# Seven products of sums for the second products of a gated layer, on one Trainium2 core

## The chip, the core and the metric

The kernel runs on one core of a Trainium2 chip. Five engines matter: TensorE (PE in the profile, its weight loads PEld), VectorE (DVE), ScalarE (ACT), GpSimd (POOL) and SyncE (SP), which here only issues DMAs. Each works through its own list of instructions in order and waits on semaphores for the others. The metric is the device time in microseconds (us) of one execution; lower is better.

## The reference

Two layers, each an attention block and a gated block, on one sequence of 2048 tokens with 448 features, all in float32:

```python
x = x + _A_ref(_layernorm(x), A_wqkv, A_wo)              # attention, 16 heads of 28
x = x + _B_ref(_layernorm(x), B_w_gate, B_w_up, B_w_down)
# the same two lines once more, with the same weights

def _B_ref(x, w_gate, w_up, w_down):                     # (448,1792), (448,1792), (1792,448)
    g = jnp.einsum("bsd,df->bsf", x, w_gate)
    u = jnp.einsum("bsd,df->bsf", x, w_up)
    h = _sigmoid(g) * u
    return jnp.einsum("bsf,fd->bsd", h, w_down)
```

## The kernel before

**Precision.** Matmuls outside the mixing of values run in float16 on pairs: a value a is kept as `hi` = a rounded to float16 and `lo` = a - hi, and a product is three matmuls, hi·hi, hi·lo and lo·hi. `split` makes such a pair with one cast on ACT and one subtraction on DVE.

**Stages of a layer.** `project` makes queries, keys and values; `attend` goes through 16 heads; `out_project` applies the output weights and adds to x; `gated` is the gated block. Everything is issued in the order of the program text (`manual_schedule`), so each engine's queue is the order of these calls. During attention of layer 0 `Prepare` also splits the weights of the gated block on DVE, a step every few key tiles (`along`), and writes them to DRAM as `gu_parts` and `dn_parts`; `FEW` and `ASIDE` say how many score tiles of each head take their exponential on DVE (`score_aside`) and not on ACT (`score`).

**The gated stage.** The tokens lie in NB = 4 blocks of W = 512, the 1792 features in NP = 7 pairs of tiles of 128 (tile p and tile p + 7). The list `seq` goes through blocks b and, inside, pairs p. For each pair `gate_and_up` makes gate and up products by a scheme of seven products (the sums of the token side are made in the `half_steps` of the block, the sums of the weight side lie in `gu_parts`): 78 matmuls of 128x256 in PSUM banks 4 to 7. The two banks `chain` are copied out by ACT in between (`on_chain`, L1319), the two banks `side` are added in by DVE (`c11_c22` L1335, `c12` L1342). Then ACT applies the sigmoid (L1346), DVE multiplies (`times`, L1349), and `split` casts and subtracts h into two pairs of 128x512 (L200, L201). The second products of the pair before (`down`, L1288 to L1290) come next on PE: for each pair 24 matmuls of 128x448 into four banks `dnp` that gather over all seven pairs of a block; at its end DVE adds them to x (L1293). So on PE the order is gate and up of pair p, second products of pair p - 1, gate and up of pair p + 1.

**Fill.** Between pairs, `run_fill` calls the steps that make the next block's token operands: statistics and scaling (`norm`, `squares`, on DVE with a little on POOL), a turn through DRAM (`store`, `gather`), then seven steps that subtract and split (`half_steps`, L354 to L376, on DVE and ACT). Two steps a pair from pair 1 on. In the last block of layer 0 the fill makes the first block of the next layer.

**Weights.** `gu_parts` of a pair are two loads of 800 KB. Some pairs stay in SBUF from block to block, others are read again (`AFTER`, `used`, issued by POOL at L1243); `dn_parts` are loaded once a layer and stay. Large tiles come from 19 slots of SBUF (`big`) that are handed out in the order in which they were given back, small ones from 12 (`qrt`).

Of the kernel before, what the change touches and what calls it, by code (L numbers as in the profile page):

```python
# [19 lines left out]
P = 128  # L20
# [6 lines left out]
NB = 4  # L27
# [12 lines left out]
XS = 2.0 ** 10  # L40
PS = 2.0 ** -13
UNIT = 32768.0
VC = 32
# [62 lines left out]
def interleaved_layers(ctx: ExitStack, tc: tile.TileContext, x_in, wqkv, wo, w_gate, w_up,  # L106
# [729 lines left out]
    class Prepare:  # L836


        def __init__(self):
            nc.vector.memset(sums[:, 3:7], 0.0)  # L840
            self.part = cpool.tile([P, 2], F32, name="part", tag="part", bufs=1)
            self.raws, self.packs = big.ring(2), big.ring(2)
            self.halves = None
            tiles = [("o", 0)] + [("d", j) for j in range(4)] + [("gu", j) for j in range(7)]
            order = [(self.measure, what) for what in tiles] + [
                (self.split, what) for what in tiles[:5] + [(w, p) for p in range(NP)
                                                            for w in ("g", "u")]]
# [22 lines left out]
        def read(self, kind, j):  # L870
            if kind in "gu" and len(kind) == 1:
                if self.halves is None:
                    self.halves = big.at(self.raws, "raws", [P, 2, 1024])
                self.next = self.halves[:, (kind == "u") * 1]
            else:
                self.next = big.at(self.raws, "raw", [P, 2048])
            if kind == "o":
                load_rows(self.view(self.next, kind), wo, 0, D, nc.gpsimd)
            elif kind == "gu":
                for i, w in enumerate((w_gate, w_up)):  # L880
                    load_rows(self.view(self.next, kind)[:, i], w, j * 2 * P, 2 * P, nc.gpsimd)
            elif kind in "gu":
                v, w = self.view(self.next, kind), {"g": w_gate, "u": w_up}[kind]
# [15 lines left out]
        def view(self, t, kind):  # L899
            if kind == "gu":  # L900
                return t.rearrange("p (w s c) -> p w s c", w=2, s=4)
            if kind in "gu":
                return t[:, 0:1024].rearrange("p (s z n) -> p s z n", s=4, z=2)
            return t[:, 0:4 * D].rearrange("p (s n) -> p s n", s=4)

        def step(self, do, what, then):
            raw = self.next
            self.write()
            if then:
                self.read(*then)  # L910
            do(raw, *what)
            if what == ("g", 0):
                big.free.append(self.raws.popleft())
# [33 lines left out]
        def sizes(self):  # L947
# [3 lines left out]
            both_back(1, 2, 3, 2.0 ** -23)  # L951
            both_back(2, 5, 6, 2.0 ** -23)
            nc.vector.tensor_scalar(back[:, 3:4], pw.bitcast(F32)[:, 4:5], 2.0 ** 41, None,
                                    op0=ALU.mult)

        def split(self, raw, kind, j):
# [22 lines left out]
            else:  # L979
                n = self.count(j)  # L980
                t = big.at(self.packs, "pack", [P, 4, 2, D], F16)
                scaled_split(t[:, 0:n, 0], t[:, 0:n, 1], v[:, 0:n], 6, nc.vector)
                self.pack = (dn_parts[j][:, 0:n], t[:, 0:n])

# [18 lines left out]
    def attend(layer, values, heads, last_values, gate, keep):  # L1003
# [133 lines left out]
        def more(g):  # L1137
            if g >= groups:
                return
            for u in main[3 * g:3 * g + 3]:  # L1140
                if u in side:
                    begin.append(side[u])
                if u % (NT * NB) == 8:
# [6 lines left out]
                    elif h == H - 1:  # L1150
                        gate.load_out()
                        gate.load_gu(0)
            score(g)
# [32 lines left out]
    def out_project(outs, gate):  # L1186
# [42 lines left out]
    class WeightsGated:  # L1229
# [3 lines left out]
        def __init__(self):  # L1233
            self.gu, self.dn = {}, []

# [3 lines left out]

        def load_gu(self, p, queue=nc.sync):  # L1240
            self.gu[p] = [big.get("gu", [P, N_SUMS, P], F16) for _ in range(2)]
            for m in range(2):
                queue.dma_start(self.gu[p][m], gu_parts[p, m])  # L1243

        def used(self, b, p):

            after = AFTER[p]
            if b == NB - 1 and (after is None or after < p):
                big.put(*self.gu.pop(p))
            elif after is not None:  # L1250
                big.put(*self.gu.pop(p))
                self.load_gu(after, nc.gpsimd)

        def load_dn(self):
            j = len(self.dn)
            n = min(4, NF - 4 * j)
            self.dn.append(big.get("dn", [P, 4, 2, D], F16))
            nc.sync.dma_start(self.dn[-1][:, 0:n], dn_parts[j][:, 0:n])

    def gated(layer, first, wt, before_next):  # L1260
        last = layer == LAYERS - 1
        gu, dn = wt.gu, wt.dn
        wt.load_dn()
        wt.load_gu(3)
        wt.load_dn()
        wt.load_gu(6)
        wt.load_dn()

        seq = [(b, p) for b in range(NB) for p in range(NP)]
        blks = [first]  # L1270
        steps = deque()
        pend = []
        accs = {}
        held = {j: min(4, NF - 4 * j) for j in range(4)}

        def down(b, p, a, hl):


            begin, end = p == 0 and a == 0, p == NP - 1 and a == 1
            if begin:  # L1280
                accs[b] = [bank(j, "dnp")[:, 0:D] for j in range(TB)]
            for j in range(TB):
                f = p + NP * (j // 2 ^ a)
                dw = dn[f // 4][:, f % 4]
                c = j if a == 0 else (j + 2) % 4
                s = slice(c * P, (c + 1) * P)
                pm = accs[b][j]
                nc.tensor.matmul(pm, hl[:, 0, s], dw[:, 0, :], start=begin, stop=False)  # L1288
                nc.tensor.matmul(pm, hl[:, 0, s], dw[:, 1, :], start=False, stop=False)  # L1289
                nc.tensor.matmul(pm, hl[:, 1, s], dw[:, 0, :], start=False, stop=end)  # L1290
                if end:
                    t = b * TB + j
                    nc.vector.scalar_tensor_tensor(x[:, t, :], pm, back[:, 2:3], x[:, t, :],  # L1293
                                                   op0=ALU.mult, op1=ALU.add)
                    if last:
                        nc.sync.dma_start(x_dst[:, t, :], x[:, t, :])
            qrt.put(hl)
            if b == NB - 1 and a == 1:
                for f in (p, p + NP):
                    held[f // 4] -= 1  # L1300
                    if not held[f // 4]:
                        big.put(dn[f // 4])

        def gate_and_up(blk, w):
# [8 lines left out]
            two = [qrt.get("two", [P, W]) for _ in range(2)]  # L1313
            lo, hi = slice(0, W // 2), slice(W // 2, W)

# [32 lines left out]
            def times(out, v):  # L1348
                nc.vector.scalar_tensor_tensor(out, v, PS, out, op0=ALU.mult, op1=ALU.mult)  # L1349

# [20 lines left out]
            qrt.put(one[1], two[1])  # L1371
            hls = []
            for h in (one[0], two[0]):
                hl = qrt.get("hhl", [P, 2, W], F16)
                split(hl[:, 0, :], hl[:, 1, :], h)
                qrt.put(h)
                hls.append(hl)
            return hls

        for b, p in seq:  # L1380
            if p == 0:
# [3 lines left out]
                elif not last:  # L1385
                    blks.append(Block(0))
                    steps.extend(blks[NB].steps())
            hls = gate_and_up(blks[b], gu[p])
            wt.used(b, p)
            if p == NP - 1:  # L1390
                blks[b].drop()
            for d in pend:
                down(*d)
            pend = [(b, p, a, hls[a]) for a in range(2)]
            for f in (2 * p, 2 * p + 1):
                if 2 <= f:
                    run_fill(steps)
                if b == NB - 1 and not last:
                    before_next(f)
        for d in pend:  # L1400
            down(*d)
        return blks[NB] if not last else None
# [35 lines left out]
    for layer in range(LAYERS):  # L1438
# [6 lines left out]
        def before_next(f, wq=wq):  # L1445
            if f == 6:
                wq.load()
# [30 lines left out]
```

## Time and profile before

| | us |
|---|---|
| median of 3 runs | 1938.38 (1937.44 to 1939.35) |
| the profiled execution | 1939.73 |
| its span, first to last instruction | 1937.9 |

Busy time of that execution: PE 1919.4 us (99%), weight loads 1321.1 (68%), DVE 1234.5 (64%), ACT 1316.6 (68%), POOL 165.4 (9%). The granted clock of TensorE is 0.997 on average.

In the rows, L12 is line 12 of the kernel. A group row gives line, engine, operation, output <- input with their shapes, the count, then busy us, mean ns of one, and the idle time in front with what ended it. A timeline row gives start, length, engine, line, operation, and in brackets the idle time before it. A window row gives the stretch, its length, then busy us with the count in brackets for PE, PEld, DVE, ACT and POOL, then the granted clock, the share of the DMA engines and GB/s. A row of DMA issues gives the count, the size of one and the median us to landing.

### The profile page before, as it was taken

The numbers are of one execution on the slowest core, as the hardware profiler recorded it, in microseconds if no ns is written. First come the engines' busy times: TensorE is split into PE (matmuls) and PEld (weight loads), VectorE is DVE, ScalarE is ACT, GpSimd is POOL, SyncE is SP. The second block draws the span as 40 slices with busy tenths as digits, with TensorE's granted clock in tenths as the row PEclk, the third lists the DMA queues.
The fourth block names the chain that finished last, engine by engine and source line by source line (L and its number), as shares of the span: only waits on it lengthen the run. The fifth ranks groups of instructions, "written<-read, shape, count | busy, mean of one in ns | idle before, by whom it ended". The sixth has DMA issues, their size and how long they took to land. (4 is left out here: it accounts for less than half of the span.)

```text
span 1937.9 us, 53581 instructions
## 1 busy us (share of the span) xinstructions
PE 1919.4 (99%) x23405; PEld 1321.1 (68%) x23405; DVE 1234.5 (64%) x2325; ACT 1316.6 (68%) x1577; POOL 165.4 (9%) x307
## 2 busy tenths in 40 slices
PE   9999999999999999999999999999999999999999
PEld 4445555556556777777744577778898777777776
DVE  7628878788655555555375477787778664655543
ACT  5559999999993343444345799999999644343432
POOL 2013322211001000000000000000000000000000
PEclk9999999999999999999999999999999999999999
DMA  5565664334216313232244321122111243333310
GB/s 171 163 203 152 185 201 127 116 89 125 64 61 241 107 69 107 75 134 78 87 125 126 98 51 32 45 50 51 36 41 65 95 176 118 107 107 97 117 50 20
DMA packets 90518, 201.53 MB, mean 104 GB/s; under 512 B 10814, under 2 KB 58014, under 8 KB 90144
## 3 DMA queue, kind: packets, MB, share of 16 engines
q1 hardware_dynamic: 65664, 111.02, 19.3%
q0 software_dynamic: 17776, 83.51, 12.9%
q8 instruction: 188, 3.08, 0.7%
q10 hardware_dynamic: 6832, 3.44, 0.7%
q14 instruction: 58, 0.48, 0.1%
HBM read 142.61 MB, written 47.98 MB: 98 GB/s over the span
## 5 line engine op out<-in xcount | busy, mean ns | idle before, releaser
L1046 ACT ACTIVATE prob_s<-sc 128x1536 f32<-128x1536 f32 x659 | 891.4, 1491 | 6.2 <-PE sc L1031 5.7
L1082 PE MATMUL acc<-prob_s,val_s 128*32 128x256 f32 (+3 forms) x7748 | 589.3, 383 | 0.0
L1031 PE MATMUL sc<-qp_s 114*32 114x512 f16 x7896 | 575.6, 380 | 4.4 <-issue 2.2
L507 PEld LDWEIGHTS <-gu_s 128*128 128x128 f16 x4368 | 427.3, 98 | 60.9 <-issue 1.7
L1031 PEld LDWEIGHTS <-qp_s 114*32 114x32 f16 x8192 | 310.6, 96 | 181.0 <-issue 80.2
L1082 PEld LDWEIGHTS acc<-prob_s,val_s 128*32 128x32 f32 x7748 | 316.0, 110 | 100.7 <-issue 6.9
L1335 DVE TENSOR_TENSOR one_q<-side,one_q 128x512 f32<-128x512 f32 x112 | 72.0, 684 | 305.8 <-PE side L507 305.6
L507 PE MATMUL chain<-xwide_s,gu_s 128*128 128x256 f16 x2016 | 247.5, 273 | 0.6 <-ACT one_q L1319 0.5
L1319 ACT COPY one_q<-chain 128x256 f32<-128x256 f32 x224 | 83.0, 373 | 205.4 <-PE chain L507 201.6
L1062 DVE SCALAR_TENSOR_TENSOR power_q<-power_q,expo_q 128x512 f32<-128x512 f32 x222 | 153.6, 692 | 7.6
L1289 PE MATMUL dnp<-dn_s,hhl_q 128*128 128x448 f16 x448 | 157.9, 352 | 0.0
L1290 PE MATMUL dnp<-dn_s,hhl_q 128*128 128x448 f16 x448 | 157.9, 352 | 0.0
L1288 PE MATMUL dnp<-dn_s,hhl_q 128*128 128x448 f16 x448 | 157.9, 352 | 0.0
L507 PE MATMUL side<-xshort_s,gu_s 128*128 128x256 f16 x1120 | 140.9, 272 | 0.3 <-DVE one_q L1335 0.3
L492 PE MATMUL qkp<-xhl_s,wqk_s 128*128 128x512 f16 x616 | 138.0, 379 | 2.2 <-DVE xhl_s L206 0.7
L1111 DVE STREAM_TRANSPOSE oturned_q<-acc 128x512 f32<-128x512 f32 x32 | 22.9, 716 | 142.5 <-PE acc L1082 142.5
L492 PEld LDWEIGHTS <-wqk_s 128*128 128x128 f16 x616 | 60.3, 98 | 72.2 <-issue 2.8
L1056 DVE TENSOR_SCALAR expo_q<-aside,base 128x512 f32<-128x512 f32 x74 | 55.4, 748 | 58.1 <-PE aside L1031 57.8
L507 PE MATMUL side<-xwide_s,gu_s 128*128 128x256 f16 x672 | 91.7, 273 | 0.0
L1319 ACT COPY two_q<-chain 128x256 f32<-128x256 f32 x112 | 41.7, 373 | 67.4 <-PE chain L507 67.4
L1082 PE MATMUL acc<-power_q,val_s 128*32 128x128 f32 (+3 forms) x276 | 86.4, 394 | 0.0
L1346 ACT ACTIVATE one_q<-one_q 128x512 f32<-128x512 f32 x56 | 35.3, 630 | 59.8 <-DVE one_q L1335 59.8
(185 smaller groups left out, 2078.8 us busy)
## 6 DMA issues: line engine op xcount, KB each, us to landing
gu_s<-gu_parts POOLq DMA_DIRECT2D x56, 800.0 KB, 4.8
qp_s<-qk_scr SPq DMA_DIRECT2D x96, 224.0 KB
gu_s<-gu_parts SPq DMA_DIRECT2D x20, 800.0 KB
qk_scr<-qkhl_q SPq DMA_DIRECT2D x56, 256.0 KB
gu_parts<-pack_s POOLq DMA_DIRECT2D x14, 800.0 KB, 3.9
xraw_s<-xt_scr SPq DMA_DIRECT2D x12, 768.0 KB
xt_scr<-xs_s SPq DMA_DIRECT2D x34, 224.0 KB
qp_s<-qk_scr SPq DMA_DIRECT2D x64, 112.0 KB
```

The costliest lines, as they stand in the source:

```text
L492: nc.tensor.matmul(pm, w, x, start=(i == 0), stop=(i == len(terms) - 1))
L507: nc.tensor.matmul(pm, a, x, start=(first and i == 0), stop=(i == len(terms) - 1), skip_group_check=True)
L1031: nc.tensor.matmul(ps[32 * j:32 * j + 32, :], hd.k[:, keys], hd.q[:, qb * W:(qb + 1) * W], start=True, stop=True, tile_position=(0, 32 * j))
L1046: nc.scalar.activation(prob[:, 0:n, :], ps[:, 0:n, :], AF.Exp, scale=exp_scale)
L1056: nc.vector.tensor_scalar(y, ps, base2[:, 0:1], -126.0, op0=ALU.mult, op1=ALU.max)
L1062: nc.vector.scalar_tensor_tensor(p, p, c[k], y, op0=ALU.add, op1=ALU.mult)
L1082: nc.tensor.matmul(acc[qb * VC:(qb + 1) * VC, s], v[:, kc % TB, h, :], probs[c * NB + qb][:, s], start=(kc == 0 and a == 0), stop=(kc == N ...
L1288: nc.tensor.matmul(pm, hl[:, 0, s], dw[:, 0, :], start=begin, stop=False)
L1289: nc.tensor.matmul(pm, hl[:, 0, s], dw[:, 1, :], start=False, stop=False)
L1290: nc.tensor.matmul(pm, hl[:, 1, s], dw[:, 0, :], start=False, stop=end)
L1319: nc.scalar.copy(to, pm)
L1335: nc.vector.tensor_tensor(one[m], side[m], one[m], op=ALU.add)
```

## The change

The second products are made by the same scheme of seven products as the first. Tokens of a block and columns of the output are halved (256 tokens, 224 columns), and a pair of feature tiles gives the two halves of the inner dimension. On the weight side `Prepare` makes four differences and writes seven operands a pair. On the token side `operands` makes four sums of h on POOL and splits all seven operands (ACT cast, DVE subtraction) into `hparts` tiles that hold a whole block. The seven products of block b - 1 then run on PE one by one (`product`, 42 matmuls of 128x224 each), product p + 1 behind the gate and up of pair p of block b for p from 1 to 5, products 0 and 1 behind pair 0, none behind pair 6 and none in block 0. Three banks are gathered in and read out by DVE after each product (`add`, `finish`). The last block's seven products stand alone at the end of the stage, in the order `TAIL`. Two pairs of `gu_parts` and three products of `dn_parts` are in SBUF at a time, and each pair and each product is loaded anew for every block, by POOL. `FEW` moves three score tiles of layer 0 from DVE to ACT, and the steps of `Prepare` stand at other key tiles.

```diff
+HS = PS / 2
-AFTER = (None, 4, 5, None, 1, 2, None)
+DN = D // 2
-FEW = "22211212121212"
+FEW = "22212121111111"
+TAIL = (0, 1, 5, 2, 6, 3, 4)
...
-    dn_parts = dpool.tile([4, P, 4, 2, D], F16, name="dn_parts")
+    dn_parts = dpool.tile([NP, P, NP, 2, DN], F16, name="dn_parts")
...
-                at += 4 if do == self.measure else 5 if what[0] in "od" else 10
+                at += 4 if do == self.measure else {"o": 5, "w": 8}.get(what[0], 7)
...
+                t1, t2, t3, t4 = [a[:, i] for a in sums for i in range(2)]
+                b11, b12, b21, b22 = [v[:, z, c:c + DN] for z in range(2) for c in (0, DN)]
+                for to, a, b in ((t1, b12, b11), (t2, b22, t1), (t3, b22, b12), (t4, b21, t2)):
+                    nc.vector.tensor_tensor(to, a, b, op=ALU.subtract)
...
-        gate.load_gu(1)
-        gate.load_dn()
-        gate.load_gu(2)
+        gate.load_gu()
...
+        def used_gu(self):
+            big.put(*self.gu.popleft())
+            if self.pairs:
+                self.load_gu(nc.gpsimd)
+
+        def used_dn(self):
+            big.put(self.dn.popleft())
+            if self.products:
+                self.load_dn(nc.gpsimd)
...
+        def operands(b, p, one, two):
+            s12, s34 = [qrt.get("hsums", [P, 2, W // 2]) for _ in range(2)]
+            a11, a22, a21, a12 = one[:, low], one[:, high], two[:, low], two[:, high]
+            for to, a, c, op in ((s12[:, 0], a21, a22, ALU.add),
+                                 (s12[:, 1], s12[:, 0], a11, ALU.subtract),
+                                 (s34[:, 0], a11, a21, ALU.subtract),
+                                 (s34[:, 1], a12, s12[:, 1], ALU.subtract)):
+                nc.gpsimd.tensor_tensor(to, a, c, op=op)
+            for k, a in ((0, a11), (4, a22), (5, a12), (1, s12[:, 0]), (2, s12[:, 1]),
+                         (3, s34[:, 0]), (6, s34[:, 1])):
+                to = place(b, p, k)
+                split(to[:, 0], to[:, 1], a)
+            qrt.put(one, two, s12, s34)
+
+        BANK = (0, 1, 0, 0, 0, 2, 1)
+        HALVES = ((0, 0), (1, 1), (0, 1), (1, 1), (1, 0), (0, 0), (0, 1))
+
+        def product(b, k, pairs=range(NP), w=None, apart=False):
+            i = 3 if apart else BANK[k]
+            begins = k in (0, 1, 5) or apart
+            ...
+            for p in pairs:
+                a = place(b, p, k)
+                for j in range(2):
+                    pm = banks_of[i][:, j * DN:(j + 1) * DN]
+                    t = slice(j * P, (j + 1) * P)
+                    for n, (x, y) in enumerate(((0, 0), (0, 1), (1, 0))):
+                        nc.tensor.matmul(pm, a[:, x, t], w[:, p, y], ...)
...
-            hls = []
-            for h in (one[0], two[0]):
-                hl = qrt.get("hhl", [P, 2, W], F16)
-                split(hl[:, 0, :], hl[:, 1, :], h)
-                qrt.put(h)
-                hls.append(hl)
-            return hls
+            return one[0], two[0]
...
-            hls = gate_and_up(blks[b], gu[p])
-            wt.used(b, p)
+            h = gate_and_up(blks[b], wt.gu[0])
+            wt.used_gu()
             if p == NP - 1:
                 blks[b].drop()
-            for d in pend:
-                down(*d)
-            pend = [(b, p, a, hls[a]) for a in range(2)]
-            for f in (2 * p, 2 * p + 1):
-                if 2 <= f:
-                    run_fill(steps)
...
+            if b > 0 and p == 0:
+                product(b - 1, 0)
+                wt.used_dn()
+                product(b - 1, 1)
+                wt.used_dn()
+                finish(b - 1, 0)
+                operands(b, p, *h)
+                finish(b - 1, 1)
+            else:
+                operands(b, p, *h)
+                if b > 0 and p < NP - 1:
+                    product(b - 1, p + 1)
+                    wt.used_dn()
+                    finish(b - 1, p + 1)
+            if p > 0:
+                run_fill(steps, 2)
...
+        for n in range(3):
+            product(b, TAIL[n], range(NP - 1), w[n])
+        for n in range(3):
+            product(b, TAIL[n], [NP - 1], w[n])
+            wt.used_dn()
+            finish(b, TAIL[n])
+        for k in TAIL[3:]:
+            product(b, k, apart=(k == 4))
+            wt.used_dn()
...
```

More of the change, by code (lines that the diff above doesn't have):

```diff
@@ L1233, in __init__ @@
         def __init__(self):
-            self.gu, self.dn = {}, []
+            self.gu, self.dn = deque(), deque()
+            self.pairs = deque(p for b in range(NB) for p in range(NP))
+            self.products = deque(list(range(NP)) * (NB - 1) + list(TAIL))
         def load_out(self):
@@ L1271, in gated @@
         steps = deque()
[L1272 to L1302, printed above, removed]
@@ new lines, in gated @@
+        BANK = (0, 1, 0, 0, 0, 2, 1)
[3 more added lines that the diff above has]
+            begins = k in (0, 1, 5) or apart
+            if begins and pairs[0] == 0:
+                banks_of[i] = bank(i, "dnp")
+            w = w or wt.dn[0]
+            for p in pairs:
[4 more added lines that the diff above has]
+                    for n, (x, y) in enumerate(((0, 0), (0, 1), (1, 0))):
+                        nc.tensor.matmul(pm, a[:, x, t], w[:, p, y],
+                                         start=(begins and p == 0 and j == n == 0),
+                                         stop=(p == NP - 1 and n == 2), skip_group_check=True)
@@ new lines, in add, with leave, finish @@
+        def add(b, i, t, c):
+            v = x[:, b * TB + 2 * t:b * TB + 2 * t + 2, c * DN:(c + 1) * DN]
+            pm = banks_of[i][:, 0:D].rearrange("p (t n) -> p t n", t=2)
+            nc.vector.scalar_tensor_tensor(v, pm, back[:, 2:3], v, op0=ALU.mult, op1=ALU.add)
+        def leave(b, t):
+            if last:
+                for j in range(b * TB + 2 * t, b * TB + 2 * t + 2):
+                    nc.sync.dma_start(x_dst[:, j, :], x[:, j, :])
+        def finish(b, k):
+            add(b, BANK[k], *HALVES[k])
+            if k == 4:
+                leave(b, 1)
+            if k == 6:
+                leave(b, 0)
@@ L1445, in before_next @@
         def before_next(f, wq=wq):
[L1446 removed]
+            if f == NF - 1:
                 wq.load()
```

92 lines of the change are left out of this document (54 added, 38 removed).

## The prediction

> **What bounds the kernel now.** I read the page first, then the gated stage by windows and the timeline of single pairs, then the groups by line and the tensor engine's (PE's) waits. PE is busy for the whole span, and in the gated stage of layer 1 for 324.74 of 325 us:
>
> ```profile
> span 1937.9 us, 53581 instructions
> PE 1919.4 (99%) x23405; PEld 1321.1 (68%) x23405; DVE 1234.5 (64%) x2325; ACT 1316.6 (68%) x1577; POOL 165.4 (9%) x307
> 1595.00:1920.00 325.00, 324.74 (x2532) 247.49 (x2531) 161.31 (x325) 131.73 (x312) 18.47 (x35) 1.00 0.27 90
> ```
>
> PE at 99% can hide gaps, since ends of matmuls are modelled, so I read starts. One pair late in layer 1 (start, length, engine, line):
>
> ```profile
> 1877.09 1.47 PE L507 MATMUL chain<-xwide_s,gu_s 128*128 128x256 f16 x12
> 1878.39 0.82 PE L507 MATMUL side<-xwide_s,gu_s 128*128 128x256 f16 x6
> ...
> 1884.51 1.25 PE L507 MATMUL side<-xshort_s,gu_s 128*128 128x256 f16 x10
> ...
> 1885.60 0.35 PE L1288 MATMUL dnp<-dn_s,hhl_q 128*128 128x448 f16 x1
> ...
> 1885.79 0.35 PE L1289 MATMUL dnp<-dn_s,hhl_q 128*128 128x448 f16 x1
> ...
> 1885.93 0.42 ACT L1346 ACTIVATE two_q<-two_q 128x256 f32<-128x256 f32 x1 [1.16 <-DVE two_q L1342]
> ...
> 1886.37 0.43 DVE L1349 SCALAR_TENSOR_TENSOR two_q<-two_q,two_q 128x256 f32<-128x256 f32 x1
> ...
> 1890.14 1.47 PE L507 MATMUL chain<-xwide_s,gu_s 128*128 128x256 f16 x12
> ```
>
> Twelve matmuls of 256 columns issue in 1878.39 - 1877.09 = 1.30 us, 0.109 each; a matmul of 448 columns takes 0.189 (1885.60 to 1885.79). The pair runs 13.05 us: 78 x 0.109 = 8.51 of gate and up, then 24 x 0.189 = 4.54 of second products, with no gap. The gate's last matmul issues to E = 1885.60; the product h is complete at 1886.37 + 0.43 = 1886.80, that is E + 1.2. The second products of the pair before run from E to 1890.14 and so cover everything that ACT and VectorE (DVE) do to finish h. Where they are missing, at the first pair of a layer, the trace shows what comes next:
>
> ```profile
> 1575.77 1.47 PE L507 MATMUL chain<-xwide_s,gu_s 128*128 128x256 f16 x12
> ...
> 1577.01 0.62 ACT L200 CAST hhl_q<-two_q 128x512 f16<-128x512 f32 x1
> 1577.08 0.82 PE L507 MATMUL side<-xwide_s,gu_s 128*128 128x256 f16 x6
> ...
> 1577.54 0.64 ACT L1319 COPY one_q<-chain 128x256 f32<-128x256 f32 x2
> ...
> 1577.95 1.25 PE L507 MATMUL chain<-xwide_s,gu_s 128*128 128x256 f16 x10
> ```
>
> One gate follows another directly. PE issues 18 matmuls (1.97 us), and the 19th needs the chain bank that ACT copies out (L1319). ACT works in order and is still casting h, so PE restarts at 1577.95 instead of 1577.73: only 0.2 us, with two casts in the way. This is the place to price in the changed kernel.
>
> **The change part by part.** *Second products.* Removed: 3 lines x 448 = 1344 matmuls of 448 columns, 1344 x 0.189 = 254 us. Added: 2 layers x 4 blocks x 7 products x 7 pairs x 2 x 3 = 2352 of 224 columns.
>
> ```profile
> L1289 PE MATMUL dnp<-dn_s,hhl_q 128*128 128x448 f16 x448 | 157.9, 352 | 0.0
> L507 PEld LDWEIGHTS <-gu_s 128*128 128x128 f16 x4368 | 427.3, 98 | 60.9 <-issue 1.7
> ```
>
> By the slope between the two intervals (0.189 - 0.109 over 192 columns) one of 224 takes 0.096, all 226: **-28 us**. If the weight load's record of 98 ns is an interval, 2352 x 0.098 = 230 and the gain is 24; if small matmuls stay at the 0.109 of the gate, it is a loss of 2. I take 0.096, as records of loads overlap matmuls throughout. The Trainium skill, "TensorE: Matmul & The Clock Gate", section "LDWEIGHTS (loading the stationary operand)", gives columns / 1.2 ns, 107 ns for 128 columns, which speaks against the change: by it the 2352 would take 251 us and the gain shrink to 3; the row of 98 ns is already below it.
>
> *Making the operands.* h was cast and subtracted in two halves (2 casts, 2 subtractions of 512 columns). Now seven operands of 256 need 7 casts on ACT, 7 subtractions on DVE and four additions on GpSimd (POOL), three of which form a chain. In the instruction order of the changed kernel all of them stand ahead of the next gate's copies on ACT, and ahead of its additions on DVE. The rows for them:
>
> ```profile
> L367 ACT CAST xwide_s<-xraw_s 128x256 f16<-128x256 f32 x12 | 4.2, 400 | 0.0
> L1319 ACT COPY two_q<-chain 128x256 f32<-128x256 f32 x112 | 41.7, 373 | 67.4 <-PE chain L507 67.4
> L928 DVE TENSOR_TENSOR sums_q<-raws_s 128x256 f32<-128x256 f32 x28 | 11.7, 419 | 0.0
> L620 POOL MEMSET val_s<- 128x256 f32 x8 | 2.7, 343 | 29.7 <-PE side L507 29.7
> L273 POOL TENSOR_SCALAR rs<-mv 128x4 f32<-128x4 f32 (+1 forms) x14 | 2.7, 195 | 305.4 <-DVE mv L270 298.9 <-DVE pw L228 6.5
> ```
>
> No row has a 256-column addition on POOL. From below it is 0.34 (the memset: one stream out). A fixed 0.195 and three streams of 0.343 - 0.195 = 0.148 give an estimate of 0.64; with a DVE subtraction of 0.42 in front of each (below) 1.06. I take **0.80**, between these two, because DVE subtracts for about half of that stretch (7 x 0.42 of some 5 us).
>
> An *open boundary* is a gate directly behind a gate. From E: h at 1.2, four additions 3.2 and hand-overs 0.1 (4.5), the last cast 0.40, the copy that PE needs 0.37: 5.3. PE has 1.97 of its own, so it stands **3.3 us**. Products now run beside pairs 1 to 5 of the next block (product p + 1) and two beside pair 0, so nothing covers the six boundaries inside block 0, nor the three from pair 6 to the next block: 9 a layer, 9 x 3.3 = 30.
>
> *The next block's preparation* ("fill", two steps a pair) stands behind the operands on the same queues:
>
> ```profile
> L371 ACT CAST xwide_s<-t_q 128x512 f16<-128x512 f32 x24 | 14.8, 616 | 10.7 <-DVE t_q L358 5.5 <-DVE t_q L354 5.2
> L376 ACT COPY xshort_s<-xshort_s 64x256 f16<-64x256 f16 x24 | 9.7, 403 | 26.7 <-DVE xshort_s L372 14.2 <-DVE xshort_s L368 12.5
> 1678.87 0.62 DVE L269 BATCH_NORM_STATS2 st<-x 128x6 f32<-128x448 f32 x1
> ...
> 1687.18 0.65 DVE L295 STREAM_TRANSPOSE xs_s<-xn_s 128x448 f32<-128x448 f32 x1
> ```
>
> On ACT, with 26.7 / 24 = 1.1 of waiting before a copy (L376): pair 2 stores, 1.4; pair 3 two casts and a wait, 1.8; pair 4 two casts of 0.616 and a wait, 1.8; pair 5 0.616 + 2 x 0.40 + 0.403 + 1.1 = 2.9; pair 6 the same and one more copy, 3.3. At open boundaries this adds in full: 11.2 in block 0 and 3.3 at the end of blocks 1 and 2, 18 a layer. Open boundaries come to 48 a layer, **+96**. At boundaries with a product, PE has 1.97 + 42 x 0.096 = 6.0 against 5.3, so 0.7 is spare and the excess over it counts: 0.7 + 1.1 + 1.1 + 2.2 = 5.1 a block, five blocks with a fill (1 and 2 in both layers, 3 in layer 0): **+26**. On DVE, norm and squares take 1687.83 - 1678.87 = 9.0 us after pair 1. In blocks with products they now also start behind the addition of the product (E + 4.03 + 0.68): done at E + 13.7, then the gate's addition 0.68, E + 14.4; PE comes to its c12 group at E + 4.03 + 7.4 = 11.4 and stands 3. Block 0 is like it, 3.7. With subtractions that wait for POOL 3.5, in seven blocks: **+25**.
>
> *Attention.* FEW moves three score tiles of layer 0 from DVE to ACT, 998 to 1001 in the main groups, one group more of 891.4 / 659 = 1.35 us on an engine that is full there: **+1.4**.
>
> ```profile
> L1046 ACT ACTIVATE prob_s<-sc 128x1536 f32<-128x1536 f32 x659 | 891.4, 1491 | 6.2 <-PE sc L1031 5.7
> ```
>
> *PE's clock.* Standing costs more than its length where the granted clock (the third number from the end) falls. Before the first scores PE issues 6 matmuls in the 3.2 us from 121.95 to 125.18, and then:
>
> ```profile
> 121.60 0.35 PE L515 MATMUL vp<-wv_s,xhl_s 128*128 128x448 f16 x1
> 122.58 0.61 PE L1031 MATMUL sc<-qp_s 114*32 114x512 f16 x6 [0.63 <-DMA qp_s<-qk_scr]
> 125.18 2.32 PE L1031 MATMUL sc<-qp_s 114*32 114x512 f16 x18 [1.99 <-issue]
> ...
> 124.00:125.00 1.00, 0.00 (x0) 0.00 (x0) 0.00 (x0) 0.00 (x0) 0.00 (x0) 0.87 0.95 303
> 127.00:128.00 1.00, 1.00 (x8) 0.28 (x3) 0.00 (x0) 1.00 (x2) 0.00 (x0) 0.50 1.03 237
> 129.00:130.00 1.00, 1.00 (x10) 0.36 (x12) 0.00 (x0) 0.05 (x1) 0.00 (x0) 1.00 1.02 278
> ```
>
> Half the clock for some 3.3 us loses 1.6. There will be 18 open boundaries and 7 stalls inside gates, all of 3.3 to 6.6 us. None falling costs 0, all 40; about a third, **+12**.
>
> *Weights.* All are read for every block: 2.4 MB in a pair with a product, 1.6 MB in block 0.
>
> ```profile
> gu_s<-gu_parts POOLq DMA_DIRECT2D x56, 800.0 KB, 4.8
> 1627.00:1628.00 1.00, 1.00 (x7) 0.49 (x5) 1.00 (x4) 0.62 (x1) 0.00 (x0) 1.00 1.01 416
> L1243 POOL DMA_DIRECT2D gu_s<-gu_parts x56 | 31.2, 557 | 330.9 <-PE side L507 250.4 <-PE chain L507 65.7 <-PE op L519 8.4
> ```
>
> At 416 GB/s 2.4 MB take 6 us of a pair of 12.6, and a load is issued a whole pair ahead: 0. What hides it is that pair; at half the rate it would still fit, in block 0 hardly. The two issues stand on POOL ahead of the additions, 2 x 0.557 from E, done before h is. The end of the layer (four products whose operands lie there) gives PE work without gates and costs nothing; its loads are issued during the first three products.
>
> *Sum.* -28 + 1.4 + 96 + 26 + 25 + 12 = +132. The profiled execution took 1939.7 us (span 1937.9), 1.3 above the median of 1938.4; from the median the forecast is **2070 us**.
>
> **The rivals.** *Cheaper additions.* Every 0.1 us of an addition is 4 x 0.1 at the some 35 places where POOL's chain ends last (18 open boundaries, 7 inside gates, some 10 covered ones), 14 us. At 0.64 the sum falls by 22, at 0.34 by up to 64, but then ACT's own seven casts of 0.40 end last and hold some 50 of it, and short stalls leave the clock alone: 2005 to 2045. For it: POOL is 9% busy. Against: no row has it read two streams. Chance 0.24.
>
> *POOL and DVE take turns.* DVE's subtractions read two operands from SBUF, as POOL's additions do. If one waits for the other, an addition costs 0.64 + 0.42 = 1.06, 35 x 4 x 0.26 = 36 more, and longer stalls lower the clock oftener: 2100 to 2125. The Trainium skill says so in "SBUF — State Buffer", section "Who interferes with whom": the port pair shared by DVE and GpSimd is locked for a whole instruction, against a DVE instruction with two SBUF inputs where the GpSimd one reads SBUF. No run shown here has the two side by side. Chance 0.25.
>
> *Late weights.* A load waits on POOL's queue behind four additions, and twice the bytes move. In block 0 a pair takes some 12 us for 1.6 MB; only at a third of 416 GB/s would they need as long, 11.5. If loads then land 1 to 2 us late in the 14 pairs of both blocks 0: 2070 to 2095. Chance 0.05.
>
> *Faster.* PE keeps the 28 us if ACT passes the next gate's copies ahead of its need. It decides at the open boundary: with 28 us against 18 of them, each may stand 1.5. But without any POOL work the casts of seven operands alone take 7 x 0.37 from about E + 0.8, and the copy ends at E + 3.8, 1.8 beyond PE's 1.97. It needs casts of about 0.3 in a row, which L367 and L1319 speak against. It would give 1938.4 - 28 + 1.4 = 1912 to 1935. Chance 0.04.
>
> **How the numbers follow.** The forecast's own case (2045 to 2100) has 0.42, cheaper additions 0.24, turns 0.25, late weights 0.05, faster 0.04. The range 2005 to 2125 takes in all but the faster case and the tails of the two beside the forecast; its ends are the additions at 0.34 and at 1.06. A difference under 0.2% (4 us) could not be told from none: faster 0.04, same 0.01 (the near end of cheaper additions), slower 0.95.
>
> **What would show it.** Right: the second products' matmuls start 0.096 apart; PE waits for ACT's copy of the chain bank (L1372 of the changed kernel) for 3 to 7 us at each gate of block 0 and at the first gate of the others, and for DVE's addition (L1388) once a block in pair 2; POOL's additions of 128x256 show between 0.6 and 1.1 us; each gated stage grows by some 60 us; slices of the gated stage show a clock under full. Wrong: matmuls of 224 columns at 0.109; boundaries under 1.5 us; PE waiting for gu_s or dn_s, a DMA; or growth in attention of layer 0 by more than 2 us.

## The result, and the profile after

The changed kernel takes 2106.19 us (median of 4 runs, 2101.9 to 2109.5), the kernel before beside it 1938.87. The ratio is 1.086, with a 95% interval of 1.083 to 1.089: slower by 167 us. The forecast was 2070 within 2005 to 2125.

The page of the changed kernel, its first lines and the row of the clock, and last the same row of the kernel before:

```profile
span 2100.1 us, 56668 instructions
...
PE 1944.8 (93%) x24437; PEld 1444.5 (69%) x24437; DVE 1423.3 (68%) x2677; ACT 1390.2 (66%) x1858; POOL 408.6 (19%) x642
...
PEclk9999999999998899999999999999999988999999
```

```profile
PEclk9999999999999999999999999999999999999999
```

PE is busy for 25 us more and stands for 137 us more. The clock, flat before, dips most in two places, which are the two blocks 0 of the gated layers. By windows (PE, weight loads, DVE, ACT, POOL, granted clock, DMA share, GB/s), the first row is layer 0's block 0, the first gate of block 1 and the first two products; the next goes from there into the first gate of block 2; the last is the end of block 3 with the products that run without gates:

```profile
612.30:739.50 127.20, 92.25 (x709) 76.30 (x708) 77.14 (x149) 53.45 (x143) 39.15 (x56) 0.85 0.40 138
739.50:827.00 87.50, 77.35 (x698) 69.43 (x697) 61.56 (x118) 38.35 (x102) 28.83 (x42) 0.96 0.48 160
...
1003.00:1066.00 63.00, 61.01 (x603) 58.07 (x602) 31.73 (x58) 19.68 (x52) 16.09 (x28) 1.00 0.45 167
```

From the first gate matmul to the next layer's first projection the stage of layer 0 takes 1065.83 - 612.28 = 453.5 us; before, it took 366.9 (613.0 to 979.9). That of layer 1, up to its last matmul, takes 442.7 and took 367.1. PE's waits in the whole run, with times and the longest, after and before:

```profile
PE chain L510 <- ACT one_q L1372: 112.3, 30, 6.8
PE side L510 <- DVE one_q L1388: 25.4, 7, 4.1
```

```profile
PE chain L507 <- ACT one_q L1319: 0.5, 2, 0.2
PE side L507 <- DVE one_q L1335: 0.3, 1, 0.3
```

Nothing waits for gu_s or dn_s; their loads take longer to land (the last column, 4.8 before) and are still in time:

```profile
gu_s<-gu_parts POOLq DMA_DIRECT2D x104, 800.0 KB, 6.0
```

And the first open boundary, by the timeline of all engines:

```profile
621.19 1.48 PE L510 MATMUL chain<-xwide_s,gu_s 128*128 128x256 f16 x12
...
622.50 0.82 PE L510 MATMUL side<-xwide_s,gu_s 128*128 128x256 f16 x6
622.56 0.77 POOL L1311 TENSOR_TENSOR hsums_q<-two_q,one_q 128x256 f32<-128x256 f32 x1 [8.62 <-DVE two_q L1402]
...
623.40 0.79 POOL L1311 TENSOR_TENSOR hsums_q<-hsums_q,one_q 128x256 f32<-128x256 f32 x1
623.53 0.94 DVE L204 TENSOR_TENSOR hparts_s<-two_q,hparts_s 128x256 f16<-128x256 f32 x1
624.15 0.90 POOL L1311 TENSOR_TENSOR hsums_q<-one_q,two_q 128x256 f32<-128x256 f32 x1
...
625.02 0.90 POOL L1311 TENSOR_TENSOR hsums_q<-two_q,hsums_q 128x256 f32<-128x256 f32 x1
...
625.95 0.40 ACT L203 CAST hparts_s<-hsums_q 128x256 f16<-128x256 f32 x1 [0.46 <-POOL hsums_q L1311]
626.26 0.64 ACT L1372 COPY one_q<-chain 128x256 f32<-128x256 f32 x2
626.68 1.47 PE L510 MATMUL chain<-xwide_s,gu_s 128*128 128x256 f16 x12 [3.36 <-ACT one_q L1372]
```

This is the chain of the prediction, link by link: h complete 1.2 us after E = 621.19, four additions to 625.92, the last cast to 626.35, the copy, and PE starts again after a stand of 3.36 us. What the prediction did not have right shows one boundary later, and where the first product runs:

```profile
638.70 2.72 PE L510 MATMUL chain<-xwide_s,gu_s 128*128 128x256 f16 x12 [3.35 <-ACT one_q L1372]
641.21 1.06 PE L510 MATMUL side<-xwide_s,gu_s 128*128 128x256 f16 x6
...
731.46 8.21 PE L1335 MATMUL dnp<-dn_s,hparts_s 128*128 128x224 f16 x84
739.51 1.47 PE L510 MATMUL chain<-xwide_s,gu_s 128*128 128x256 f16 x12
```

After this second stand, of the same length, twelve matmuls take 641.21 - 638.70 = 2.51 us, not 1.31: half the clock. The matmuls of 224 columns run 84 in 739.51 - 731.46 = 8.05 us, 0.0958 each.

### The profile page after: what moved, and what is told of

It reads as the page before. It is cut to its first block, busy times and chain, and to the rows that moved or that the text cites. A ratio compares the mean times of both kernels' runs of the same rounds, so it can differ in the third digit from the quotient of the medians.

```text
span 2100.1 us, 56668 instructions
## 1 busy us (share of the span) xinstructions
PE 1944.8 (93%) x24437; PEld 1444.5 (69%) x24437; DVE 1423.3 (68%) x2677; ACT 1390.2 (66%) x1858; POOL 408.6 (19%) x642
## 5 line engine op out<-in xcount | busy, mean ns | idle before, releaser
L510 PEld LDWEIGHTS <-gu_s 128*128 128x128 f16 x4368 | 447.6, 102 | 215.4 <-issue 144.2
L1103 PEld LDWEIGHTS acc<-prob_s,val_s 128*32 128x32 f32 x7782 | 322.0, 110 | 96.9 <-issue 7.4
L510 PE MATMUL chain<-xwide_s,gu_s 128*128 128x256 f16 x2016 | 277.0, 293 | 112.3 <-ACT one_q L1372 112.3
L1335 PE MATMUL dnp<-dn_s,hparts_s 128*128 128x224 f16 x2352 | 238.0, 263 | 0.0
L1335 PEld LDWEIGHTS <-hparts_s 128*128 128x128 f16 x2352 | 229.6, 99 | 4.0
L510 PE MATMUL side<-xshort_s,gu_s 128*128 128x256 f16 x1120 | 144.2, 277 | 25.4 <-DVE one_q L1388 25.4
L1083 DVE SCALAR_TENSOR_TENSOR power_q<-power_q,expo_q 128x512 f32<-128x512 f32 x213 | 147.4, 692 | 7.2
L203 ACT CAST hparts_s<-hsums_q 128x256 f16<-128x256 f32 x224 | 88.9, 404 | 95.8 <-POOL hsums_q L1311 95.8
L204 DVE TENSOR_TENSOR hparts_s<-hsums_q,hparts_s 128x256 f16<-128x256 f32 x224 | 132.4, 648 | 2.3 <-ACT hparts_s L203 2.3
L1265 POOL DMA_DIRECT2D gu_s<-gu_parts x104 | 57.3, 552 | 254.8 <-PE side L510 167.9
L510 PE MATMUL side<-xwide_s,gu_s 128*128 128x256 f16 x672 | 103.8, 297 | 0.0
```

Source lines behind the costliest of these rows:

```text
L203: nc.scalar.copy(hi, raw)
L204: nc.vector.tensor_tensor(lo, raw, hi, op=ALU.subtract)
L510: nc.tensor.matmul(pm, a, x, start=(first and i == 0), stop=(i == len(terms) - 1), skip_group_check=True)
L1083: nc.vector.scalar_tensor_tensor(p, p, c[k], y, op0=ALU.add, op1=ALU.mult)
L1103: nc.tensor.matmul(acc[qb * VC:(qb + 1) * VC, s], v[:, kc % TB, h, :], probs[c * NB + qb][:, s], start=(kc == 0 and a == 0), stop=(kc == N ...
L1265: queue.dma_start(self.gu[-1][m], gu_parts[p, m])
```

## The experiments

The theory: the four additions, the casts behind them and the next block's preparation stand in front of the next gate's copies; PE stands there, and its clock falls with it. The rivals: POOL's chain is hidden behind ACT's own casts; POOL and DVE take turns; the slow matmuls have another cause than standing; the weights' transfers.

**Additions on DVE.**

```
-                nc.gpsimd.tensor_tensor(to, a, c, op=op)
+                nc.vector.tensor_tensor(to, a, c, op=op)
```

> The four additions of h's quarters move from POOL to VectorE (0.42 us each there by the like rows, instead of 0.72 to 0.90). Theory (POOL's chain of additions ends last at the open boundaries, ACT's casts wait for it, and the next gate's copies wait behind the casts): the first open boundary of a layer falls from 3.35 us to about 1.7, the waits for ACT's copy from 112 us to about 90, the waits in the gate for VectorE in pair 2 of block 0 rise from 2.5 to about 4 to 5 because VectorE has four more instructions; time 2070 to 2090 us. Rival (what ends last there is ACT's own seven casts and the hand-overs, POOL is hidden): waits for ACT as before, those for VectorE longer, 2106 to 2120. Rival (POOL and VectorE take turns): as in the theory, and VectorE's subtractions of 256 columns fall from 0.65 to 0.42 us.

Measured: 2067.93 us, ratio to before 1.0665 (1.0647 to 1.0683). PE's waits, then DVE's subtractions in the groups by line, and last the same group of the changed kernel with two of POOL's additions:

```profile
PE chain L510 <- ACT one_q L1372: 83.9, 28, 6.1
PE side L510 <- DVE one_q L1388: 29.4, 7, 5.5
```

```profile
L204 DVE TENSOR_TENSOR hparts_s<-hsums_q,hparts_s 128x256 f16<-128x256 f32 x224 | 79.6, 416 | 0.0
```

```profile
L204 DVE TENSOR_TENSOR hparts_s<-hsums_q,hparts_s 128x256 f16<-128x256 f32 x224 | 132.4, 648 | 2.3 <-ACT hparts_s L203 2.3
L1311 POOL TENSOR_TENSOR hsums_q<-two_q,hsums_q 128x256 f32<-128x256 f32 x56 | 49.5, 884 | 0.0
L1311 POOL TENSOR_TENSOR hsums_q<-hsums_q,one_q 128x256 f32<-128x256 f32 x56 | 43.7, 780 | 4.4
```

POOL's chain did end last: with the additions on DVE 38 us go, slightly more than expected, and the wait at the first open boundary falls from 3.36 to 1.42 us. The waits in the gate grow, as expected. POOL does slow DVE: a subtraction takes 0.65 beside POOL's additions and 0.42 without them. The rival of turns expected the same, so this run does not tell it from another slowing.

**No additions.**

```
-                nc.gpsimd.tensor_tensor(to, a, c, op=op)
+                pass
...
-            for k, a in ((0, a11), (4, a22), (5, a12), (1, s12[:, 0]), (2, s12[:, 1]),
-                         (3, s34[:, 0]), (6, s34[:, 1])):
+            for k, a in ((0, a11), (4, a22), (5, a12), (1, a21), (2, a11),
+                         (3, a22), (6, a12)):
```

> Leaves out the four additions on POOL: operands 1, 2, 3 and 6 are made from quarters of h instead of sums. Prices POOL's chain. Theory (prediction: 1.8 us of an open boundary remain, from seven casts on ACT in a row): first open boundary 1.7 us, waits for ACT from 112 us to 70 to 80, for VectorE 25 to 20; the subtractions on VectorE fall to 0.42 us; with less clock lost 2035 to 2060 us. Rival (POOL's additions lie beside ACT's casts and cost nothing): 2100 to 2106.

Measured: 2027.03 us, ratio 1.0453 (1.0435 to 1.0470).

```profile
PE chain L510 <- ACT one_q L1372: 61.3, 27, 4.9
PE side L510 <- DVE one_q L1388: 22.5, 7, 4.2
```

Making the sums costs 79 us of the 167, and the time is below the span expected. PE still waits for 84 us. At the first open boundary, where only the casts stand in the way, it stands for 1.07 us, less than the 1.7 expected; the longest waits, up to 4.9 us, are where the preparation stands there too.

**Idle matmuls where PE stands**, n of them ahead of second(0) and m ahead of c12(0), by tables of pairs:

```
+        def hold(blk, w, n):
+            if n:
+                pm = bank(3, "hold")
+                for i in range(n):
+                    nc.tensor.matmul(pm[:, low], w[0][:, i % 6, :], blk.wide[:, 0, 0, 0, :],
+                                     start=(i == 0), stop=(i == n - 1))
...
+            hold(blk, w, n)
             second(0)
...
+            hold(blk, w, m)
             c12(0)
```

> Idle matmuls of 256 columns into an unused bank are placed in front of the matmul that waits, 16 to 62 of them, as many as fill the wait seen in the changed kernel; they add nothing to the result. Theory (the about 50 us that are neither waits nor matmuls at full speed are the tensor engine's clock, which falls because the engine stands): the granted clock goes from 0.968 back to 0.995 or more, first groups after a wait take 1.47 us and not 2.72, and the time falls by 40 to 55 us to 2051 to 2066. Rival (those matmuls are slow for another cause, such as reading weights that are still being written, or the transfers): groups behind the waits stay at 2.7 us, 2106 or, where a filling is too long, up to 2115.

Measured: 2066.10 us, ratio 1.0658 (1.0640 to 1.0676). The page's row of the clock, the group of idle matmuls and the waits that are left:

```profile
PEclk9999999999999999999999999999999999999999
```

```profile
L1364 PE MATMUL hold<-xwide_s,gu_s 128*128 128x256 f16 x1271 | 144.5, 273 | 0.0
```

```profile
PE chain L510 <- ACT one_q L1382: 6.2, 10, 1.5
PE side L510 <- DVE one_q L1398: 3.0, 2, 1.5
```

1271 matmuls that compute nothing make the kernel 40 us faster. DVE, ACT and POOL do exactly what they did (the same 0.65 for a subtraction), so these 40 us are PE's clock alone. As the price of the clock it is rather a low figure: the filling and the waits left add up to 1271 x 0.109 + 9 = 148 us, somewhat more than the stands they replace.

**The same, with 14 fewer in each place.**

```
         def hold(blk, w, n):
+            n = max(0, n - 14)
```

> As the kernel with idle matmuls in front of the waits, with 14 fewer in each place, so that the tensor engine stands about 1.5 us and not 0 in each. Asks from which length on a stand costs clock. Theory (the runs so far: stands up to 1.8 us were followed by full speed, of those from 2.0 us on most by half speed): clock 0.995 or more, first groups after a stand 1.47 us, time as with the full filling, 2062 to 2070 us. Rival (every stand costs clock, in proportion): clock about 0.983, 2080 to 2090 us.

Measured: 2072.42 us, ratio 1.0687 (1.0671 to 1.0704). The waits, and two of them in PE's timeline:

```profile
PE chain L510 <- ACT one_q L1383: 46.4, 36, 1.9
PE side L510 <- DVE one_q L1399: 14.0, 7, 3.0
```

```profile
628.32 1.47 PE L510 MATMUL chain<-xwide_s,gu_s 128*128 128x256 f16 x12 [1.61 <-ACT one_q L1383]
...
649.98 2.17 PE L510 MATMUL side<-xshort_s,gu_s 128*128 128x256 f16 x10 [3.03 <-DVE one_q L1399]
```

PE now stands 43 times for 60 us in all. Behind the 41 stands of up to 1.93 us every group runs at full speed; the two slow ones are behind the two stands of 3.0 us (ten matmuls took 2.17, and 2.29 in layer 1, instead of 1.25). The gated stages take 433.6 and 425.0 us, with the full filling 434.6 and 424.6. The time is 2 us over the span expected. The 6 us that separate the two kernels lie, in the profiled runs, between the gated layers, in the projection of layer 1, where PE stood once for 4.3 us; why is open.

Length alone does not decide. In the clock record of the changed kernel's trace the clock changes only at points of a raster of 3.413 us. The first stand of 3.36 us has such a point inside it, 1.31 us on one side and 2.04 on the other, and the clock stays; the second, of 3.35, puts 2.93 us into one window, and the next one has half the clock (window rows as before, two for each stand):

```profile
624.64:628.05 3.41, 1.37 (x13) 1.23 (x13) 2.23 (x4) 1.73 (x5) 2.33 (x4) 1.00 0.27 54
628.05:631.46 3.41, 3.41 (x33) 3.06 (x32) 0.69 (x2) 1.12 (x3) 0.00 (x0) 1.00 0.99 400
...
634.88:638.29 3.41, 0.47 (x5) 0.28 (x3) 3.41 (x5) 1.53 (x5) 2.98 (x4) 1.00 0.00 0
638.30:641.70 3.40, 3.00 (x15) 2.13 (x15) 3.26 (x10) 1.24 (x5) 0.00 (x0) 0.50 0.00 0
```

The traces of all eleven kernels, from 200 us on, agree: 126 such windows at full clock were followed by one at half, and PE was idle in each of them for 2.03 us or more; in the others it was idle for 2.04 us at most. By these figures a single stand of up to 2.0 us costs no clock, one of more than 4.1 us always does, and in between it depends on where it falls.

**Late operands.** Casts and subtractions move into the next gate, behind its copies; some(i, j) issues the next i casts and j subtractions of the pair before:

```
             first(1)
+            some(2, 2)
             apart(0)
...
             second(1)
+            some(2, 2)
             apart(1)
...
             third(1)
+            some(3, 0)
             c11_c22(0)
             c11_c22(1)
+            some(0, 2)
             sigmoid(one[0], one[0])
...
+            some(0, 1)
             c12(0)
```

> The additions stay on POOL where they were, but the seven casts and subtractions of a pair are issued inside the next pair's gate, two behind each pair of copies of the chain bank and three behind the third (subtractions likewise), instead of ahead of that gate's first copy. Theory (the open boundary's price is the order on ACT: copies behind casts behind POOL's additions): the first two open boundaries of a layer vanish (3.35 to under 0.3 us), those with a fill step shrink to the fill's own 0.5 to 3.3 us, the waits in the gate for VectorE stay or grow to 4 to 5 us; waits in all 65 to 85 us of 138, less clock lost, 2000 to 2035 us. Rival (casts in the middle of the gate delay the copies there as much as they did ahead of it): waits move into the gate, 2080 to 2106 us.

Measured: 2024.29 us, ratio 1.0440 (1.0423 to 1.0458).

```profile
PE chain L510 <- ACT one_q L1383: 47.7, 22, 4.8
PE side L510 <- DVE one_q L1399: 30.8, 7, 5.2
```

The same instructions in another order are 82 us faster, and the waits at the first two open boundaries are gone. What is left stands in pairs with preparation, at open boundaries for up to 4.8 us where 3.3 were expected.

**No preparation of the next blocks.**

```
-        blks = [first]
+        blks = [first] * NB
```

> Leaves out the preparation of blocks 1 to 3 of each gated layer (all blocks use the operands of block 0; the next layer's first block is still prepared). Prices the fill, which the prediction put at 18 a layer in open boundaries, 26 in covered ones and 25 in the gates. Theory: waits of 138 us fall by 65 to 75, all open boundaries stand 3.2 to 3.4 us, no wait for VectorE in the gate outside the last block of layer 0; with less clock lost 2010 to 2030 us. Rival (the longer waits of pairs 4 to 6 come from the operands getting slower from pair to pair, such as weights or transfers): these stay over 5 us, 2060 us or more.

Measured: 2010.42 us (one run).

```profile
PE chain L510 <- ACT one_q L1372: 62.6, 22, 3.3
PE side L510 <- DVE one_q L1388: 4.1, 1, 4.1
```

```profile
627.44 2.72 PE L510 MATMUL chain<-xwide_s,gu_s 128*128 128x256 f16 x12 [3.35 <-ACT one_q L1372]
```

The waits fall by 71 us, and each open boundary stands 3.34 to 3.35 us, whatever its pair: an open boundary costs the same 3.3 everywhere, and all above that (up to 6.8) was the preparation.

**No rereading of weights.**

```
-            big.put(*self.gu.popleft())
-            if self.pairs:
-                self.load_gu(nc.gpsimd)
+            self.left_gu -= 1
+            tiles = self.gu.popleft()
+            if self.left_gu > len(self.gu):
+                self.gu.append(tiles)
+            else:
+                big.put(*tiles)
```

and likewise for the products' weights.

> Leaves out the rereading of weights: the first two pairs' gate and up weights and the first three products' weights are used in turn for all pairs and products of a layer. Prices the transfers and their issues on POOL. Theory (the weights cost nothing): 2100 to 2108 us, the same waits for ACT and VectorE within 3 us. Rival (the issues ahead of POOL's additions, or the doubled traffic, delay the operands): 10 us less or more, 2060 to 2095 us, and POOL's additions or VectorE's subtractions become shorter.

Measured: 2103.91 us, ratio 1.0844 (1.0828 to 1.0859), against 1.0834 to 1.0886 for the changed kernel.

```profile
PE chain L510 <- ACT one_q L1379: 113.2, 31, 7.1
PE side L510 <- DVE one_q L1395: 25.0, 7, 4.1
```

The transfers cost nothing that can be measured.

**Everything spread.** The additions stay behind the gate; casts and subtractions move into the next gate (in blocks 0 and 2 as four wider ones); the preparation is cut into single steps, in the middle of the gates of block 0 and ahead of the product's addition later.

```
+            some = operands(b, p, *h)
+            ks = () if b == 0 or p == NP - 1 else (0, 1) if p == 0 else (p + 1,)
+            for k in ks:
+                product(b - 1, k)
+                wt.used_dn()
+            at('e')
+            for k in ks:
+                finish(b - 1, k)
...
             third(1)
+            at('t')
```

operands() issues POOL's additions at once; at() issues what a table gives for its place in the gate, casts and subtractions of the pair before and steps of the next block's preparation.

> All parts of the change are kept, but nothing stands ahead of a gate's first copies any more: POOL's additions are issued right behind the gate, the casts and subtractions of a pair inside the next gate (in blocks 0 and 2 as four wider instructions each instead of seven), the next block's preparation one step at a time in the middle of the gates of block 0 and, in the later blocks, beside the product ahead of its addition, norm and squares apart. Theory (all that the change loses is the order on ACT and VectorE and the clock that falls with it; the matmuls alone are worth -28): waits in the gated layers under 25 us in both, clock 0.995 or more, time 1939 - 28 + 1 + 15 to 25 = 1925 to 1940 us, faster than before. Rival (in block 0, where no product runs, VectorE and ACT have more work than the 8.5 us of a gate, the more so as VectorE's subtractions stretch beside POOL): the pairs of block 0 take 10 us and more, 1945 to 1965 us.

Measured: 1939.03 us, ratio 0.9997 (0.9988 to 1.0006), no difference from before. PE's largest group of waits:

```profile
PE chain L509 <- ACT one_q L1392: 11.7, 12, 3.3
```

With 7.2 us behind DVE the waits are 18.9 us, and the clock is 0.997, as the theory had it; the time is at the upper end of the theory's span, and no gain is left. The gated stages take 365.9 and 363.1 us. One wait of 3.3 us in layer 0 was a cast for the next block whose tile had not yet landed, 19 us after its store was issued.

**The same, with the preparation a pair earlier.**

```
-        FILLS = {(0, 's'): 1, (1, 'f'): 1, (1, 's'): 1, (2, 'f'): 1, (2, 's'): 1, (2, 'e'): 1,
-                 (4, 's'): 1, (4, 'x'): 1, (5, 's'): 1, (5, 'x'): 1, (6, 's'): 1, (6, 'x'): 1}, ...
+        FILLS = {(0, 'b'): 1, (0, 'f'): 1, (0, 'e'): 1, (1, 'f'): 1, (1, 's'): 1, (1, 'e'): 1,
+                 (4, 'f'): 1, (4, 's'): 1, (5, 'f'): 1, (5, 's'): 1, (6, 's'): 1, (6, 'x'): 1}, ...
```

The keys are the pair and the place in its gate, the values how many of the 13 steps are issued there in block 0 (twelve in all).

> As the kernel with everything spread over the gates, but the next block's preparation starts a pair earlier in block 0 (norm and two tiles of squares in and behind the first gate, whose VectorE is idle) and its operands come after the gathered tile has landed, which in layer 0 took 19 us from the store's issue and held a gate up for 3.3 us. Theory (what still separates that kernel from 1939 - 28 is waits of 19 us and the holes around them): waits under 11 us, no wait over 1.5 us, time 1927 to 1934 us, 0.994 to 0.997 of before. Rival (VectorE and ACT are full in block 0, so that work only moves from one wait to another): 1936 to 1940 us.

Measured: 1930.83 us, ratio 0.9961 (0.9948 to 0.9975): 0.4% less than the kernel before, a small difference, but its interval leaves out 1.

```profile
span 1928.0 us, 56522 instructions
...
PEclk9999999999999999999999999999999999999999
```

```profile
PE chain L509 <- ACT one_q L1392: 9.4, 13, 1.1
PE side L509 <- DVE one_q L1408: 4.7, 6, 1.0
PE chain L509 <- DMA gu_s<-gu_parts: 0.8, 1, 0.8
PE side L509 <- DVE two_q L1415: 0.7, 2, 0.3
```

Waits are 15.6 us where under 11 were expected; the longest is 1.1. The gated stages take 361.8 and 362.4 us, against 366.9 and 367.1 before.

## Why the prediction was right, and where it was not

Direction and mechanism were right, and the time lies in the range; it lies above the forecast's own case of 2045 to 2100, and the main reason is one term. The sum against the profiled executions (2100.1 - 1937.9 = 162.2 us):

- *Second products*, forecast -28: 2352 x 0.0958 = 225.3 against 254.0, **-28.7**. Neither 0.098 nor 0.109 was seen, and the weight load's 107 ns, by which the gain would have been 3, does not pace these matmuls.
- *Open and covered boundaries*, forecast 96 + 26 = 122: **112.3**, of which 91 in the 18 open ones. A plain open boundary was forecast at 3.3 and measured at 3.35. The additions were taken at 0.80 and took 0.78 to 0.88 on average.
- *Inside gates*, forecast 25 in seven blocks: **25.4**, seven waits. That the sum is so near is luck: in blocks 0 they were forecast at 3.7 and took 2.3 and 2.6, in the others 3 and took 4.1.
- *Weights*, forecast 0: within the 2 us that separate the two medians.
- *Attention*, forecast +1.4: not to be seen. The gated layer 0 begins at 612.3 after and 613.0 before, and kernels that are alike up to there begin between 612.1 and 614.9.
- *PE's clock*, forecast +12: **40** by the kernel with idle matmuls. This is the step that failed: "None falling costs 0, all 40; about a third, +12". The price of one fall was about right, the share was not: after 27 of the 29 stands over 2.3 us the clock fell, and 27 x 1.6 = 43. Why a third the prediction does not say.

Add the waits, less 0.8 of before, and some 6 us that the wait column leaves out (a stand is counted from a matmul's modelled end, 0.27 after its start, where the next would have started after 0.11; 37 x 0.16). Then -28.7 + 136.9 + 6 = 114, and 48 are left for the clock, where the filling showed 40 as a low figure. The trace bears the 48 out: added up matmul by matmul, those of the gated stages start 50 us later in all than at 0.109 and 0.0958 apiece. The gated stages grew by 87 and 76 us, where some 60 each were forecast.

*The rivals.* The measured time lies in the span given for "POOL and DVE take turns", 2100 to 2125, but not by its mechanism, an addition of 1.06. Alone they take 0.72 and 0.42 (their shortest); beside each other an addition takes up to 0.91 and a subtraction 0.95. From 622.56 to 625.92 POOL finished four additions while DVE finished three subtractions, 3.36 us; in turns of whole instructions these need 4 x 0.72 + 3 x 0.42 = 4.1. The Trainium skill, "SBUF — State Buffer", section "Who interferes with whom", calls the port pair that they share an exclusive lock; held for whole instructions it would give those 4.1, and the trace does not show it in that form. But turns in some form are not refuted: side by side the two go in step, one addition and one subtraction every 0.87 us, where alone an addition follows another after 0.68 to 0.81 and a subtraction after 0.34. So this rival was right that they hold each other up, and had its size too large. The time above the forecast came from the clock. *Cheaper additions*: not so. It said that ACT's own casts would still hold some 50; with no additions at all the waits for ACT are 61.3, but there the preparation has a part in it, and where the casts stand alone PE waits 1.07 us and not the 1.8 of the prediction, so the nearness is in part luck. *Late weights*: refuted by leaving them out. *Faster*: it needed ACT to pass the copies ahead of the operands; the changed kernel doesn't, and of the two with everything spread, which do, the second came to 1930.83, inside that rival's 1912 to 1935, the first to 1939.03.

## What to carry to other kernels

Where a product is moved away from the place that it covered, look in every in-order queue for what stands ahead of the next use of the accumulation banks; here nearly the same work, in smaller steps and issued some microseconds later, turned 1.086 into 0.996. Price a stand of the tensor engine twice, once for its length and once for the clock, as soon as it is over 2 us; shorter single stands cost only their length. A saving of 29 us of matmuls pays only when the operands' extra work on other engines finds a place inside the gates.

## What the runs showed of the hardware

- Stands of up to 1.9 us left the clock alone, 41 times out of 41 in one run. Of the 29 stands from 2.3 to 6.8 us in the changed kernel 27 were followed by matmuls at 0.21 us where 0.109 is the rule, for up to 5.9 us. The other two had a point of the clock's 3.413 us raster inside them, with at most 2.04 us on one side. The Trainium skill, "TensorE: Matmul & The Clock Gate", section "HAM oscillation — how this bites in real kernels", warns of gaps over some 3.4 us; here gaps of 2.3 to 3.3 us were enough.
- Filling a stand with matmuls that compute nothing made a kernel 40 us faster, although the other engines worked no faster.
- Two engines that read two operands each from SBUF stretch each other: DVE's subtraction of 256 columns from 0.42 to up to 0.95 us, POOL's addition from 0.72 to up to 0.91. Whether the reads are the reason was not tested by itself.
